# Sliding-window attention and feed-forward on one core: attention sinks laid into the preceding block's rows, with first-layer halves, an earlier W2 load and earlier crossbar transposes

## The chip, the cores and the metric

The kernel runs on one core of one Trainium2 chip. The metric is the device time of one execution in microseconds (us). Most executions agree within 0.3%; the kernel before takes 227.49 us (median of three runs, 226.96 to 227.76). A run counts as slow when it is over 1.5% above the fastest of its kernel.

## The reference, cut to what matters

Attention with a window of 128 keys and four sink keys that every query sees, then a layer norm, two matrix products with a ReLU between them, and a residual:

```python
batch, n_heads, seq, head_dim = (4, 8, 768, 64)      # n_sink 4, window 128
is_sink   = pos[None, :] < n_sink
rel       = pos[:, None] - pos[None, :]
keep      = is_sink | ((rel >= 0) & (rel < window))
a         = softmax(where(keep, q @ k.T / sqrt(64), -1e9))
x         = (a @ v), heads side by side               # 4 x 768 x 512
xn        = (x - mean) / sqrt(var + 1e-6) * g_ln
out       = x + relu(xn @ w_ch1) @ w_ch2               # 512 -> 2048 -> 512
```

## The kernel before

The 768 rows of each of four batches are cut into six blocks of 128: blocks 0 to 5 are batch 0, 18 to 23 batch 3. Four blocks form a group for the dense part (first layer `ph`, second layer `pc`). A query block sees its own keys and those of the block before it, and the window fits exactly: query row i of a block still sees key row j of the preceding block if j > i. From the third block of a batch on, the four sinks lie outside both blocks, so they get matmuls of their own: scores `pk`, an exponential, and two products per half block (line 496):

```python
if len(slots) > len(halves):                    # a sink block: 8 more score matmuls
    for h2 in range(2):
        for hp in range(4):
            nc.tensor.matmul(P["pk", t][32*hp:32*hp+32, h2, :], lhsT=ks_of[b][:, h2, hp, :],
                             rhs=qkT[t][:, 0, hp, :], start=(h2 == 0), stop=True, ...)
...
if r >= 2:                                      # and 2 more products per half block (L496)
    for h2 in range(2):
        nc.tensor.matmul(po.rearrange(...)[:, :, h2, :], lhsT=ES[t][:, h2, :], rhs=vs_t[b].rearrange(...), ...)
```

A planner inside the kernel takes tasks with estimated costs, dependencies and priorities and fixes each engine's instruction order before the kernel runs; each engine then works through its order and cannot overtake. All input loads are issued by POOL in one chain, block by block:

```python
def load(fn, land, take=(), desc=1024):
    i = plan.add({"POOL": 0.88}, [], fn, (0,), take=take, land=land, after=last_load[0], desc=desc)
    last_load[0] = i
    return i
...
DTR = set(range(8, NT))          # blocks whose transposes go through the DMA crossbar
SUBS = {0: [(0, 2), (2, 4)]}     # group 0's first layer in halves of two blocks
W2AT = 6                         # W2 is loaded ahead of block 6
for t in range(4, NT):
    if t == W2AT:
        for c in range(4):
            load_w2(c)
    load_block(t)
...
n = 8 * (t - 4) - 16             # scores of block t wait for the n-th piece of dense work
```

The softmax here doesn't subtract the row's maximum and nothing guards it: scores larger than these inputs give would overflow.

Of the kernel before, what the change touches and what calls it, by code (L numbers as in the profile page):

```python
# [14 lines left out]
class Planner:  # L15
# [16 lines left out]
    def run(self, free, warm_until):  # L32
# [15 lines left out]
        dma_free = free["DMA"]  # L48
        order = []
        queued = []  # L50
        while ready:
# [37 lines left out]
            if e == "PE":  # L89
                gaps[i] = start - free[e] if start < warm_until else 0.0  # L90
# [3 lines left out]
            if t["land"] is not None:  # L94
                dma_free = max(dma_free, start + 1.5) + t["land"]
                end = dma_free + (0.6 if t["lag"] is None else t["lag"])
                if t["desc"]:
                    queued.append((dma_free, t["desc"]))
# [15 lines left out]
    @staticmethod  # L114
    def room(queued, desc, ring=4096):

        for at, d in reversed(queued):
            desc += d
            if desc > ring:
                return at  # L120
        return 0.0

    def emit(self, order):
        for i, e, slots in order:
            self.gap = self.gaps.get(i, 0.0)
            self.tasks[i]["emit"](e, *slots)
# [3 lines left out]
def kernel(  # L130
# [35 lines left out]
    RINGS = dict(pa=4, ps=2, ld=LDN, qk=QKN, ks=2, vs=2, e=8, es=3, xc=4, xn=4, h1=32, ot=4)  # L166
# [14 lines left out]
    def warm(bank_):  # L181

        for _ in range(int(plan.gap * WARM / .056)):
# [22 lines left out]
    ks_t = [consts.tile([128, 2, 4, 32], BF16, name=f"ks_{i}") for i in range(2)]  # L206
    xt = [consts.tile([128, DM], BF16, name=f"xt_{t}") for t in range(NT)]
# [10 lines left out]
    def make_masks():  # L218
        v_ = nc.vector
        nc.gpsimd.iota(iota_d, pattern=[[1, 128]], base=0, channel_multiplier=-1)  # L220
        nc.gpsimd.iota(iota_h, pattern=[[-32, 4]], base=0, channel_multiplier=1)
        v_.tensor_scalar(ident, iota_d, 0.0, None, op0=ALU.is_equal)
# [28 lines left out]
    last_load = [None]  # L251

    def load(fn, land, take=(), desc=1024):
        i = plan.add({"POOL": 0.88}, [], fn, (0,), take=take, land=land, after=last_load[0], desc=desc)
# [58 lines left out]
    P = {}  # L313
    def w0(e, s):
# [6 lines left out]
    def opening():  # L321
        plan.add({"PE": .1}, [], w0, (0, -1, 0), take=[("pa", "w0", 0)])
        D["mb"] = plan.add({"DVE": .45}, [d_q[0]], make_masks_b, (0, 0, 1))
        D["mc"] = plan.add({"DVE": 1.3}, [d_q[0]], make_masks_c, (0, 1, 5))

# [4 lines left out]
    def block(t):  # L330
# [4 lines left out]
        split = t in SPLIT  # L335

# [20 lines left out]
        qk_readers = n_s(t) + (0 if last else n_s(t + 1)) + (1 if r == 0 else 0)  # L357
# [59 lines left out]

        s_ = []
        for halves in (((0,), (1,)) if t in SPLIT_S else ((0, 1),)):
            cost = .22 * nkb + .43 * nkb * (t in MPE)  # L420
            sink = r >= 2 and halves[-1] == 1
            x_ = plan.add({"PE": cost * len(halves) / 2 + .15 + SINK * sink},
                          d_c[t] + (d_c[t - 1] if r else []) + ([D["mb"]] if t in MPE and r else [])
                          + ([d_ks[b]] if sink else []), sc(halves),
# [7 lines left out]
        for half in range(2):  # L432
# [7 lines left out]
            def mk(e, half=half):  # L440
                m = (mask_zero, mask_one)[r] if r < 2 else mask_std
# [7 lines left out]
        if r == 0:  # L449
# [6 lines left out]
            d_ks[b] = plan.add({"DVE": .3}, d_c[t], mks, (0, t + 2, 0), take=[("ks", ("ks", b), 4)],  # L456
                               drop=[("qk", t)])
            vs_d = []
            for half in range(2):
                hs = slice(4 * half, 4 * half + 4)  # L460

                def pv_(e, s, *s2, half=half, hs=hs):
                    if s2:
# [5 lines left out]
                              take=[("pa", ("pv", b, half), 1)] + ([("vs", ("vs", b), 8)] if half == 0 else []))  # L469
# [9 lines left out]
        a_deps = [d_v[t]] + ([d_v[t - 1]] if r else [])  # L479
        if r >= 2:  # L480
# [7 lines left out]
        for half in range(2):  # L488
            def av(e, s, half=half):
# [4 lines left out]
                if r >= 2:  # L494
# [4 lines left out]
                for hh in range(4):  # L499
                    h = 4 * half + hh  # L500
                    nc.tensor.matmul(po[:, hh, :], lhsT=ee[:, h % 2, hh // 2, 0, :], rhs=vn[:, t, h, :],  # L501
                                     start=(r < 2 and hh == 0), stop=(r == 0), skip_group_check=True)
                    if r > 0:
# [3 lines left out]
            a = plan.add({"PE": (.12, .25, .37)[min(r, 2)]}, a_deps + [ms[half]], av, (0, t, 5),  # L507
                         take=[("pa", ("po", t, half), 1)],
                         drop=[("e", t, half)] + ([("es", t), ("vs", b)] if r >= 2 else []))

            def nm(e, half=half):
                po = P["po", t, half]
                rc = small.tile([128, 4], FP32, name="rc")
# [8 lines left out]
            ns.append(plan.add({"DVE": .60}, [a], nm, (0, t, 6), drop=[("po", t, half)]))  # L522
# [10 lines left out]
        def st(e):  # L533
            if ti == 0:
                mvg[g] = small.tile([128, 4, 2], FP32, name="mvg")
            st_ = small.tile([128, 6], FP32, name="st")
            nc.vector.bn_stats(st_, xt[t])  # L537
            nc.vector.bn_aggr(mvg[g][:, ti, :], st_)
# [195 lines left out]
```

## Time and profile before

| before | value |
|---|---|
| time, median | 227.49 us |
| profiled span, clock | 225.4 us, 1.00 |
| TensorE needed work, counted | 208.6 us |
| lost before the end of the last matmul | 12.5 us, of it 11.25 before 26.5 us |
| tail after the last matmul | 4.2 us |
| DVE busy / POOL busy | 135.0 / 76.0 us |

"Needed work" is the running sum of what each matmul group costs in an unbroken stream; "lost" is the real start of a group minus that sum. This pair is used throughout, because TensorE's busy share also counts warm-up matmuls. In the profile, PE is TensorE, PEld its weight loads, DVE VectorE, ACT ScalarE, POOL GpSimd, and SPq and POOLq are the queues from which SyncE and GpSimd issue transfers. The lines themselves are in the prediction.

### The profile page before, as it was taken

Reading aid. Unit: us, or ns where it says so; the run is one execution under the profiler, and the core shown is the slowest. Engines: PE = TensorE matmul, PEld = TensorE weight load, DVE = VectorE, ACT = ScalarE, POOL = GpSimd, SP = SyncE. Lnnn points to the kernel's source line nnn. Section 1 sums busy time; section 2 is a strip of 40 time slices with the busy share of each in tenths; the row PEclk is TensorE's granted clock in tenths of the full one; section 3 lists DMA queues with packets and bytes.
Section 4 is the critical chain, followed back from the end, with each engine's and each line's share of the span. In section 5 each row is a group of like instructions: output and inputs, shape, how many; then the busy total and the mean of one; then the engine's idle time right before and its main releaser. Section 6 shows DMA issues by size and latency. Waiting matters only on the chain.

```text
span 225.4 us, 4783 instructions
## 1 busy us (share of the span) xinstructions
PE 217.0 (96%) x1921; PEld 121.0 (54%) x1948; DVE 135.0 (60%) x398; ACT 104.0 (46%) x166; POOL 76.0 (34%) x92
## 2 busy tenths in 40 slices
PE   8999999999999999999999999999999999999992
PEld 7766787655455554455555544454555544444440
DVE  5777998779577988863756873654854712100121
ACT  2386788344367731167641258633077600376000
POOL 7994366691695242933088000100000010000000
PEclk9999999999999999999999999999999999999999
DMA  7999999999999999999989994203221021200111
GB/s 43 139 157 206 182 184 209 166 173 192 218 150 129 144 140 189 175 185 191 94 103 158 168 209 88 51 17 102 71 48 23 3 70 47 93 0 3 47 71 69
DMA packets 108709, 26.52 MB, mean 118 GB/s; under 512 B 101520, under 2 KB 105616, under 8 KB 108688
## 3 DMA queue, kind: packets, MB, share of 16 engines
q0 software_dynamic: 79104, 13.64, 81.7%
q1 hardware_dynamic: 29584, 12.59, 30.1%
q8 instruction: 15, 0.25, 0.4%
q14 instruction: 6, 0.05, 0.1%
HBM read 27.27 MB, written 6.29 MB: 149 GB/s over the span
## 4 chain that ended last, share of the span: by engine, by line
PE 81%; DMA 8%; POOL 5%; DVE 3%; issue 1%; ACT 0%; POOLq 0%; ACTq 0%
PE ph L603 34%; PE pc L634 34%; PE ps L406 5%; DMA w1s<-in_moe_w_ch_dram 4%; DMA qkT<-qkn 3%; PE po L501 2%; PE po L504 2%; POOL qkn L267 2%; POOL vn L275 2%; POOL qkn L272 2%; PE po L496 2%; PE pk L413 1%; PE pt L347 1%; DVE xt L517 1%; DVE w1s L299 1%
## 5 line engine op out<-in xcount | busy, mean ns | idle before, releaser
L603 PE MATMUL ph<-xnt,w1s 128*128 128x512 bf16 (+1 forms) x434 | 88.9, 348 | 1.0 <-DVE h L617 0.3
L634 PE MATMUL pc<-w2s,h 128*128 128x512 bf16 x371 | 87.0, 379 | 1.1 <-issue 0.5
L619 ACT ACTIVATE h<-ph 128x512 bf16<-128x512 f32 (+1 forms) x84 | 45.8, 546 | 53.8 <-PE ph L603 52.1
L603 PEld LDWEIGHTS <-w1s 128*128 128x128 bf16 x448 | 41.5, 98 | 35.4 <-ACT h L619 0.5
L634 PEld LDWEIGHTS <-h 128*128 128x128 bf16 x384 | 35.8, 98 | 39.1
L435 ACT ACTIVATE e<-ps 128x1024 bf16<-128x1024 f32 (+1 forms) x48 | 43.7, 951 | 12.5 <-PE ps L406 12.5
L646 DVE SCALAR_TENSOR_TENSOR ot<-pc,rsg,xt 128x512 f32<-128x512 f32 x24 | 17.9, 747 | 38.9 <-PE pc L634 38.9
L548 POOL TENSOR_TENSOR rsg<-ve,eps_half 128x4 f32<-128x4 f32 x6 | 6.2, 1028 | 82.0 <-DVE ve L546 82.0
L267 POOL DMA_DIRECT2D qkn<-in_q_dram x24 | 21.9, 910 | 14.9 <-DMA qkT<-qkn 13.1
L444 DVE TENSOR_TENSOR e<-e,mask_std 128x1024 bf16<-128x1024 bf16 x28 | 18.9, 684 | 10.9 <-ACT e L435 10.9
L617 DVE TENSOR_SCALAR h<-ph 128x512 bf16<-128x512 f32 (+1 forms) x28 | 15.9, 570 | 13.7 <-PE ph L603 13.6
L272 POOL DMA_DIRECT2D qkn<-in_k_dram x24 | 21.7, 903 | 2.8 <-DMA w2s<-in_moe_w_ch_dram 1.4
L275 POOL DMA_DIRECT2D vn<-in_v_dram x24 | 21.8, 912 | 1.8 <-DMA w1s<-in_moe_w_ch_dram 1.8
L517 DVE SCALAR_TENSOR_TENSOR xt<-po,rc 128x256 bf16<-128x256 f32 x48 | 20.4, 425 | 1.7
L501 PE MATMUL po<-vn,e 128*128 128x65 bf16 x192 | 17.1, 193 | 0.1
L537 DVE BATCH_NORM_STATS2 st<-xt 128x6 f32<-128x512 bf16 x24 | 16.4, 684 | 0.0
L406 PEld LDWEIGHTS <-qkT 64*128 64x128 bf16 x352 | 9.9, 94 | 10.4 <-issue 7.8
L406 PE MATMUL ps<-qkT 64*128 64x128 bf16 x352 | 14.7, 218 | 0.7 <-DMA qkT<-qkn 0.4
L482 ACT ACTIVATE es<-pk 128x256 bf16<-128x256 f32 x16 | 6.1, 383 | 19.9 <-PE pk L413 19.8
L514 DVE RECIPROCAL rc<-po 128x4 f32<-128x4 f32 x48 | 8.5, 178 | 11.3 <-PE po L504 10.4
L501 PEld LDWEIGHTS <-e 128*128 128x128 bf16 x192 | 14.0, 97 | 2.1 <-DVE e L444 0.5
L504 PE MATMUL po<-vn,e 128*128 128x65 bf16 x160 | 14.9, 193 | 0.0
(66 smaller groups left out, 146.2 us busy)
## 6 DMA issues: line engine op xcount, KB each, us to landing
out_dram<-ot SPq DMA_DIRECT2D x24, 256.0 KB, 2.5
qkn<-in_q_dram POOLq DMA_DIRECT2D x24, 128.0 KB, 7.1
qkn<-in_k_dram POOLq DMA_DIRECT2D x24, 128.0 KB, 6.8
vn<-in_v_dram POOLq DMA_DIRECT2D x24, 128.0 KB, 7.6
w1s<-in_moe_w_ch_dram POOLq DMA_DIRECT2D x4, 512.0 KB, 10.3
w2s<-in_moe_w_ch_dram POOLq DMA_DIRECT2D x4, 512.0 KB, 10.7
qkT<-qkn SPq DMA_TRANSPOSE x16, 7.2
xnt<-xc SPq DMA_TRANSPOSE x16, 5.6
```

What stands on the lines that cost most here:

```text
L267: nc.gpsimd.dma_start(qn[t][:, 0], q[b, :, rows, :].rearrange("h p d -> p h d"))
L272: nc.gpsimd.dma_start(qn[t][:, 1], k[b, :, rows, :].rearrange("h p d -> p h d"))
L275: nc.gpsimd.dma_start(vn[:, t, :, 0:64], v[b, :, rows, :].rearrange("h p d -> p h d"))
L406: nc.tensor.matmul(ps[:, h2, hh, kb, :], lhsT=qkT[t - kb][rows, 1, hp, :], rhs=qkT[t][rows, 0, hp, :], start=(hh == 0 and kb == 0 and t no ...
L435: nc.scalar.activation(E[t, half][:, :, :, 0:nkb, :], P["ps", t, half][:, :, :, 0:nkb, :], AF.Exp, scale=scale)
L444: nc.vector.tensor_mul(ee[:, :, 0:w], ee[:, :, 0:w], m[:, 0:w].unsqueeze(1).to_broadcast([128, 4, w]))
L501: nc.tensor.matmul(po[:, hh, :], lhsT=ee[:, h % 2, hh // 2, 0, :], rhs=vn[:, t, h, :], start=(r < 2 and hh == 0), stop=(r == 0), skip_grou ...
L504: nc.tensor.matmul(po[:, hh, :], lhsT=ee[:, h % 2, hh // 2, 1, :], rhs=vn[:, t - 1, h, :], start=False, stop=True, skip_group_check=True)
L517: nc.vector.scalar_tensor_tensor(xt[t][:, 256 * half:256 * half + 256].rearrange("p (h d) -> p h d", h=4), in0=po[:, :, 0:64], scalar=1.0, ...
L603: nc.tensor.matmul(ph, lhsT=w1s[:, j, 128 * ht:128 * (ht + 1)], rhs=xnt[g][:, j, cols], start=(j == 0), stop=(j == NDM - 1))
L619: nc.scalar.activation(o, i, AF.Relu)
L634: nc.tensor.matmul(P["pc", t], lhsT=h1[g, ht][:, 128 * ti:128 * (ti + 1)], rhs=w2s[:, ht, :], start=(ht == 0), stop=(ht == NH1 - 1))
```

## The change

Intent: for blocks 14 to 17 and 20 to 23 (`FOLD`), write the four sink keys and values over rows 0 to 3 of the preceding block, once that block no longer needs them, and open the mask for these rows. Then the ordinary matmuls do the sinks' work, and `pk`, its exponential and the products of L496 go away. The price: query row 0 loses keys 1 to 3 of the preceding block, row 1 keys 2 and 3, row 2 key 3. These six pairs per head and block are computed separately: 27 small loads on POOL fetch the rows (`fq`, `fk`, `fv`), a chain of small DVE operations forms corrections (`fc`), three small transfers spread them (`fcb`), and DVE adds them to the first three rows of the weighted sum. Beside that, group 1's first layer goes in halves, W2 is loaded one block earlier, blocks 6 and 7 use the crossbar for their normalised rows, and the pacing changes.

The diff holds four more things: the planner's own model of landings and costs, smaller rings of buffers (`xn` 2 for 4, `h1` 20 for 32), another count of warm-up matmuls, and the layer norm's row statistics, which ACT may now take in place of DVE.

```diff
+    def fetch(i, b):                                    # row i, batch b: three loads on 4 partitions each
+        at = slice(12 * i + 4 * (b - 1), 12 * i + 4 * b)
+        def f(e):
+            nc.gpsimd.dma_start(fq[at], q[b, :, 256:768, :].rearrange("h (r x) d -> x r h d", x=128)[i])
+            for to, src in ((fk, k), (fv, v)):
+                nc.gpsimd.dma_start(to[at].rearrange("r h p d -> r h (p d)"), src[b, :, 129:641, :]...)
+        fetched.append(load(f, .35, desc=96 * 3, cost=1.2))
+    def corrections():                                  # 6 score steps, exp on ACT, mask, 3 + 3 value steps
+        d = step(.2, fetched, mask)
...
+        if fold:                                        # sinks over the preceding block's rows 0 to 3
+            nc.vector.tensor_copy(qkT[t - 1][:, 1, :, 0:4], kss_of[b])
+            nc.vector.tensor_copy(vn[0:4, t - 1], vn[0:4, t - r])
...
+                if fold:
+                    nc.vector.tensor_add(po[0:3], po[0:3], fcb[:, t - RB - 2 * b, 4 * half:4 * half + 4, :])
...
-        v_ = d_var[t] = plan.add({"DVE": .87}, ...
+        v_ = d_var[t] = plan.add({"DVE": .87, "ACT": 1.1}, ...
...
-    DTR = set(range(8, NT))
+    DTR = set(range(6, NT))
-    SUBS = {0: [(0, 2), (2, 4)]}
+    SUBS = {0: [(0, 2), (2, 4)], 1: [(0, 2), (2, 4)]}
-    W2AT = 6
+    W2AT = 5
+    FOLD = 12
+    FETCH = 14
...
+        if t == FETCH:                                  # ahead of block 14's load, in the one chain of loads
+            for b in range(1, B):
+                for i in range(3):
+                    fetch(i, b)
         load_block(t)
...
-        n = 8 * (t - 4) - 16
+        n = 9 * (t - 4) - 24
```

## The prediction

> **What bounds the kernel now.** I read the page's busy shares first, then the busy time of the engines by stage, then the chain that ended last and the timeline of TensorE, and then I counted TensorE's needed work, because a busy share alone doesn't say whether the work is needed. First the page, then three stages (columns after the stretch: its length, then busy us of PE, PEld, DVE, ACT and POOL with instructions in brackets, clock, DMA share, GB/s):
>
> ```profile
> PE 217.0 (96%) x1921; PEld 121.0 (54%) x1948; DVE 135.0 (60%) x398; ACT 104.0 (46%) x166; POOL 76.0 (34%) x92
> ```
>
> ```profile
> 0.00:26.50 26.50, 24.80 (x334) 18.89 (x335) 19.66 (x76) 15.26 (x24) 20.18 (x29) 1.00 1.52 145
> 26.50:60.00 33.50, 32.72 (x355) 22.38 (x359) 28.28 (x83) 18.24 (x35) 18.75 (x22) 1.00 1.88 180
> 60.00:180.00 120.00, 118.44 (x1054) 61.28 (x1069) 80.68 (x231) 60.45 (x92) 36.04 (x41) 1.00 1.20 120
> ```
>
> PE is the only full engine from 26.5 us on; DVE is at 84% of 26.5 to 60 and 67% of 60 to 180. What one group of matmuls costs in the stream is its piece in the chain (start, us, what), since the next group starts right behind it:
>
> ```profile
> 43.53 1.73 PE pc L634 x8
> 45.26 0.22 PE px L559 x4
> 49.52 0.11 PE pv L466
> 51.82 7.83 DMA qkT<-qkn
> 60.31 0.23 PE pk L413 x8
> 63.23 0.12 PE po L496 x2
> 65.68 0.55 PE ps L406 x16
> ```
>
> So 216 ns for a 512-column matmul, 0.22 us for four transposes, 0.23 for the eight sink scores (pk), 0.12 for the two sink products of a half block (L496), 0.55 for a block's scores, which are also entered some 0.1 us late (312 ns instead of 216 from the last wide matmul before them). Counted over TensorE's whole program: first layer 320 x 216 + 128 x 109 ns = 83.1 us; second layer 384 x 216 ns = 82.9; scores 12.6 and entering them 2.6; masks by matmul 3.0; weighted sums 352 x 30 ns = 10.7; sink scores 16 x 0.225 = 3.6; sink products 32 x 0.118 = 3.8; q and k transposes 64 x 56 ns = 3.6; transposes of the normalized rows 32 x 56 ns = 1.8; sink value spreads 8 x 0.11 = 0.9. The sum is 208.6 us. The last matmul ends at 221.2, so about 12.5 us are lost, and the tail after it is 4.2.
>
> Where the 12.5 lie I see by laying this running sum against the starts in the timeline: at the matmul below 15.3 us of needed work are done, so 11.25 are already lost; at 38.95 it is 0.34 more, at 59.69 another 0.5 (block 8's transposed q and k came late; the 7.83 us above), and from there to the end some 0.2. **The opening is bound by loads and latency, everything after it by the amount of TensorE work.**
>
> ```profile
> 26.52 2.78 PE L603 MATMUL ph<-xnt,w1s 128*128 128x256 bf16 x24 [0.28 <-DVE h L617]
> ...
> 59.69 0.62 PE L406 MATMUL ps<-qkT 64*128 64x128 bf16 x16 [0.45 <-DMA qkT<-qkn]
> ```
>
> **What the Trainium skill says.** "Trainium Kernel Development and Optimization", Performance Expectations, warns that matmul busy time says little about the distance to the best, as matmuls are pipelined; I agree here, 96% also counts warm-up matmuls, and that is why I counted work. "TensorE: Matmul & The Clock Gate", Part 1, gives N / 2.4 GHz plus about 2.5 ns for a warm matmul, so 215.7 ns at 512 columns; the trace has 216, and halves of 256 columns cost 109, so splitting a first layer in halves costs TensorE under 0.3 us in 128 matmuls. The same part says that a busy array keeps its clock and an idle one loses it after a few us; here the granted clock is 1.00 in all three stages. "DMA: Bandwidth & Descriptors", Issuing engines are not separate DMA queues, says that transfers from all issuers share the same 16 engines; the 7.83 us of a transpose under loads, against 3.0 us for the quickest one of the same kind in this trace, agree.
>
> **The change part by part.**
> Sinks: for blocks 14 to 17 and 20 to 23 the four sink keys and values are written over the first four rows of the preceding block, whose mask then lets them pass, and three rows get a correction. Eight blocks lose 0.225 + 2 x 0.118 = 0.46 us of TensorE each: 3.7 us. Batches 2 and 3 have no old-style block left, so 4 of the 8 value spreads go: 4 x 0.11 = 0.45 us. ACT loses 8 x 0.38 us of sink exponentials. It adds on DVE: a 3 x 260 add per half block, estimated at 0.42 us from the 128 x 260 multiply out of PSUM (0.424), 16 times, 6.7 us; key and value copies, estimated 0.15 and 0.3, eight times, 3.6; the corrections, about a dozen 512-element fp32 operations which I estimate at 0.65 (the output operation of that width takes 0.747) plus small ones, 8.5 us. It saves about 3 us of spreads and sink key copies. DVE goes from 135 to some 150 of about 221 us. That is under the bound, beside TensorE's work.
> Loads: 27 more small loads stand on POOL between the loads of blocks 13 and 14. A 1024-row load takes 0.91 us of POOL, a 512-row one 0.745, so I estimate 0.4 to 0.7 for 32 rows: 11 to 19 us.
> Crossbar from block 6: in the instruction order only the normalized rows of blocks 6 and 7 move; q and k of these stay on TensorE. 8 x 56 ns = 0.45 us less.
> First layer of group 1 in halves: 64 matmuls of 216 become 128 of 109, no cost on TensorE; 16 more evacuations on ACT or DVE at about 0.2 us of fixed cost each, beside other work. It lets the layer start before blocks 6 and 7 are through.
> W2 behind block 4: the packet records show loads of blocks 0 to 3 until about 15.4 us, W1 to 25.7, blocks 4 and 5 to 30.9, W2 to 41.2. Now W2 ends at about 38.6 and block 5 at 41.2. Group 0's second layer begins at a running sum of 28.0 us, with 11.3 lost at 39.3, and block 5's transposes at 42.8: both just behind their data. I expect no gain and no stall.
> Opening: fewer warm-up matmuls stand before the first transposes (3 instead of 18), but the first layer waits for W1, whose first quarter was scaled from 19.7 us on in both. More attention is now done ahead of it (11.2 against 10.6 us), so up to 0.6 us less is lost; I take 0.4.
>
> Sum: needed TensorE work 208.6 - 3.7 - 0.45 - 0.45 = 204.0, with small order effects 204.2; lost 12.5 - 0.4; new stalls in the middle 0.4; tail 4.2. The span is 204.2 + 12.1 + 0.4 + 4.2 = 220.9 us. The time exceeds the profiled span by 227.45 - 225.4 = 2.05. I put it at 222.9; as the stall at block 8 may go (its transposes stand behind an output store that now comes 2.5 us earlier, worth 0.4), I settle on 222.5 us, 2.2% less.
>
> **The rivals.**
> (1) The small loads are slow. The corrections start on DVE behind block 5's output, at a running sum of 74.9, about 86.5 us. The fetches can begin when block 13 is loaded, about 66.5 (in the kernel before POOL issued block 14 there). At 0.4 us each they end at 77, at 0.65 at 84, both in time; at 0.9 at 91, and DVE, which takes its work in order, would stand some 6 us in front of block 13's masks, and block 14 would be loaded late for its scores at about 100.6. TensorE would lose 2 to 5 us: 225 to 227. For it: POOL's 0.745 for 512 rows shows a large fixed part. Against: the interval from 66.5 to 86.5 holds them at up to 0.7.
> (2) DVE becomes the bound: the fold lengthens the path from weighted sum to freed PSUM bank from 0.67 to about 1.1 us, and the one group of corrections is 8.5 us in one stretch. For it: DVE was at 84% before 60 us. Against: the fold lies after 100 us, where it was under 67%. It would make 223.5 to 225.
> (3) The crossbar in the middle or at the end is late: block 23's normalized rows are needed 7 us after its last weighted sum (running sum 169.75 to 176.6) instead of about 16. The chain there is about 2.2 us of DVE and 2.4 to 5.6 us of transpose, so 0 to 1 us lost.
> (4) The opening gains more than I think, since its 11 lost us are the largest reserve: if the first layer starts 1 us sooner, 221.5.
>
> **Range and chances.** The certain part is 4.6 us of TensorE work, to about 222.9 with nothing else; the opening can add up to 1.5 us of gain, the rivals take 1 to 5. So 220.5 to 224.9 us, 8 in 10. The 2% line is at 222.94, close above my number: faster by over 2% 0.60, within 2% 0.38, slower 0.02.
>
> **What would show it.** TensorE's groups: pk from 128 to 64, L496's from 64 to 32, pv from 8 to 4, px from 32 to 24, and the last matmul's end 4 to 5 us sooner, with the stream as gapless after 60 us as before. DVE at about 150 us busy. The small loads at 0.4 to 0.7 us each on POOL, done before 87 us. A DVE idle before the corrections, ended by a load, would prove rival 1; TensorE idle ended by DVE's normalization rival 2; TensorE idle near 188 us ended by a transpose rival 3. I am wrong if TensorE loses over 2 us more after 60 us than now, or if the opening shifts by over 1.5 us.

## The result, and the profile after

The changed kernel takes **238.92 us** (median of four runs, 237.05 to 240.99), against 227.52 us for the kernel before on the same chip. The ratio is 1.0477 (95% interval 1.0411 to 1.0543): slower by 4.8%, where 2.2% faster was predicted. Ratios are the mean time of one kernel's fast runs over the mean of the other's fast runs in the same rounds, so they are not quite the ratio of the medians quoted beside them.

The profiled run is the slowest of the four (240.99 us, span 239.2) and carries the mark slow. The other three have spans of 235.3 to 237.5 us and granted clocks of 0.976 to 0.978, against 0.968. The readings below are therefore confirmed further down on a fast run of nearly the same kernel ("The change's layout, every other part undone"), which shows the largest of the stops.

The page of the changed kernel (busy us, share, instructions; then the tenths of 40 slices of about 6 us):

```profile
PE 216.2 (90%) x1869; PEld 124.0 (52%) x1892; DVE 139.1 (58%) x422; ACT 113.2 (47%) x200; POOL 92.5 (39%) x120
...
PE   8799999998999799419949999999999999999993
...
PEclk9999999999999999956997999999999999999998
```

PE is busy for almost the same time as before, although the work fell: the 17th and 18th slice (about 96 to 108 us) are at 4 and 1 tenths, and the granted clock falls to 5 and 6 tenths in the 18th and 19th, so the matmuls that follow take twice as long and count as busy. The same by stages, with the columns that the prediction explains:

```profile
0.00:26.50 26.50, 24.12 (x328) 18.31 (x329) 18.46 (x77) 15.10 (x24) 19.86 (x30) 1.00 1.51 145
26.50:60.00 33.50, 32.55 (x355) 22.63 (x356) 25.81 (x78) 19.82 (x41) 19.45 (x23) 1.00 1.93 174
60.00:90.00 30.00, 27.45 (x334) 20.45 (x334) 23.10 (x75) 17.90 (x36) 15.15 (x22) 1.00 1.68 137
90.00:130.00 40.00, 27.59 (x181) 12.49 (x183) 20.83 (x54) 14.10 (x23) 26.17 (x33) 0.83 1.48 117
130.00:180.00 50.00, 49.53 (x366) 24.26 (x372) 29.26 (x90) 24.17 (x42) 10.86 (x12) 1.00 1.18 127
```

For the stretch of 90 to 130 us the kernel before has:

```profile
90.00:130.00 40.00, 39.48 (x342) 20.26 (x346) 26.03 (x73) 17.05 (x26) 19.34 (x22) 1.00 1.72 155
```

There PE issued 342 recorded matmuls in 39.48 us at full clock; now 181 in 27.59 us at 0.83. Everything that went wrong on a large scale lies here. In needed work and lost time, the changed kernel stands at 204.3 us of needed work, as predicted. Lost are 10.69 us at 26.3 us (0.56 less than before), 11.57 at 59.5 us, 14.70 at 91.4, 23.73 at 107.05, and 31.1 at the end. Between 91 and 129 us it loses 16.1: a stop of 9.03 at 107, 2.2 at half clock behind it, a stop of 3.20 at 125, and 1.7 at half clock behind that.

Who waited for whom (engine, line, waited for, total us, times, longest):

```profile
DVE fk L383 <- DMA fv<-in_v_dram: 11.2, 1, 11.2
...
PE po L601 <- DVE e L533: 8.9, 1, 8.9
...
DVE po L615 <- DMA fcb<-fc: 5.4, 1, 5.4
...
PE ph L714 <- DVE xt L620: 3.0, 1, 3.0
```

DVE stands 11.2 us before the first correction because the small loads that it reads have not landed: the last `fk`, issued at 98.68, lands at 101.39. (The profile names an `fv` load, which shares the wait but lands at 102.37 only.) Behind the corrections in DVE's fixed order stands block 13's mask, for which TensorE waits 8.9 us. Later DVE waits 5.4 us for the spread corrections, and TensorE, whose PSUM bank is held by block 14's sum until then, 3.0 us. DVE's and then TensorE's timeline show it (start, us, engine, line, what, idle before):

```profile
90.31 0.15 DVE L376 TENSOR_SCALAR mask_c<-iota_c 36x3 f32<-36x3 int32 x1
101.66 0.68 DVE L383 TENSOR_TENSOR fk<-fk,fq 36x512 f32<-36x512 f32 x1 [11.20 <-DMA fv<-in_v_dram]
...
106.27 0.67 DVE L533 TENSOR_TENSOR e<-e,mask_one 128x1024 bf16<-128x1024 bf16 x1
```

```profile
107.00 0.23 PE L601 MATMUL po<-vn,e 128*128 128x65 bf16 x1 [8.85 <-DVE e L533]
...
107.43 6.49 PE L714 MATMUL ph<-xnt,w1s 128*128 128x512 bf16 x19
...
115.51 3.63 PE L714 MATMUL ph<-xnt,w1s 128*128 128x512 bf16 x16
```

The 19 recorded matmuls behind the stop take 6.49 us, the 16 a little later 3.63: starts lie 426 ns apart instead of 216 until the clock returns.

And POOL's timeline shows the 27 small loads:

```profile
67.67 0.65 POOL L365 DMA_DIRECT2D fq<-in_q_dram  x1
...
70.83 0.59 POOL L367 DMA_DIRECT2D fv<-in_v_dram  x1 [1.92 <-DMA qkn<-in_q_dram]
75.06 0.59 POOL L365 DMA_DIRECT2D fq<-in_q_dram  x1 [3.64 <-DMA qkn<-in_k_dram]
...
82.48 0.59 POOL L367 DMA_DIRECT2D fk<-in_k_dram  x1 [3.15 <-DMA vn<-in_v_dram]
...
99.26 0.59 POOL L367 DMA_DIRECT2D fv<-in_v_dram  x1
99.84 0.95 POOL L295 DMA_DIRECT2D qkn<-in_q_dram  x1
```

Issuing one takes 0.59 us, within the 0.4 to 0.7 that the prediction estimated. But the 27 take from 67.67 to 99.85, 32.2 us: 16 us of issuing and 16 us of waiting. Each wait ends when the load eight issues earlier lands, so the first ones end with block loads and not with small ones: the issue at 70.83 waited for block 12's queries, issued at 59.97 and landed at 70.55, the one at 75.06 for block 12's keys, landed at 74.77. The program has eight semaphores in turn for POOL's loads, so at most eight are under way. Of the 16.3 us of waiting, 10.6 end with loads of blocks 12 and 13, which took 10.6 to 15.4 us to land, and 5.7 with small loads, of which the first 15 took 7.5 to 14.8 us and the last 12 took 2.7 to 6.3. So the eight places let through about one load per 1.2 us (32.2 / 27). Block 14's load, issued at 66.56 us before, now comes at 99.84.

### The profile page after: what moved, and what is told of

It is laid out like the page before. It is cut to its first block, busy times and chain, and to the rows that moved or that the text cites. A ratio compares the mean times of both kernels' runs of the same rounds, so it can differ in the third digit from the quotient of the medians.

```text
span 239.2 us, 4774 instructions
## 1 busy us (share of the span) xinstructions
PE 216.2 (90%) x1869; PEld 124.0 (52%) x1892; DVE 139.1 (58%) x422; ACT 113.2 (47%) x200; POOL 92.5 (39%) x120
## 4 chain that ended last, share of the span: by engine, by line
PE 64%; DMA 24%; POOL 7%; issue 2%; SPq 1%; DVE 1%; ACT 0%; POOLq 0%; DVEq 0%
PE pc L745 27%; PE ph L714 25%; DMA vn<-in_v_dram 6%; DMA qkT<-qkn 5%; DMA fk<-in_k_dram 4%; DMA fcb<-fc 4%; PE ps L484 4%; DMA qkn<-in_k_dram 3%; DMA qkn<-in_q_dram 2%; PE po L601 2%; POOL qkn L295 2%; PE pt L425 1%; PE ps L475 1%; PE po L604 1%; POOL fv L367 1%
## 5 line engine op out<-in xcount | busy, mean ns | idle before, releaser
L714 PE MATMUL ph<-xnt,w1s 128*128 128x256 bf16 (+1 forms) x506 | 92.9, 334 | 3.3 <-DVE xt L620 3.0
L745 PE MATMUL pc<-w2s,h 128*128 128x512 bf16 x367 | 86.5, 379 | 0.9 <-issue 0.2
L730 ACT ACTIVATE h<-ph 128x512 bf16<-128x512 f32 (+1 forms) x95 | 48.4, 511 | 45.9 <-PE ph L714 44.7
L714 PEld LDWEIGHTS <-w1s 128*128 128x128 bf16 x512 | 48.6, 99 | 36.5 <-issue 4.3
L659 POOL TENSOR_TENSOR rsg<-ve,eps_half 128x4 f32<-128x4 f32 x6 | 6.7, 1118 | 67.0 <-DVE ve L657 65.6
L601 PEld LDWEIGHTS <-e 128*128 128x128 bf16 x192 | 14.3, 99 | 12.8 <-DVE e L533 9.3
L728 DVE TENSOR_SCALAR h<-ph 128x256 bf16<-128x256 f32 (+1 forms) x33 | 15.5, 476 | 7.3 <-PE ph L714 6.8
L533 DVE TENSOR_TENSOR e<-e,mask_one 128x1024 bf16<-128x1024 bf16 x22 | 14.7, 684 | 5.8 <-ACT e L524 5.8
L604 PEld LDWEIGHTS <-e 128*128 128x128 bf16 x160 | 11.3, 99 | 2.3 <-issue 0.3
L615 DVE TENSOR_TENSOR po<-po,fcb 3x260 f32<-3x260 f32 x16 | 6.7, 421 | 7.4 <-DMA fcb<-fc 5.4
```

The source lines that it names most:

```text
L601: nc.tensor.matmul(po[:, hh, :], lhsT=ee[:, h % 2, hh // 2, 0, :], rhs=vn[:, t, h, :], start=(not sinks and hh == 0), stop=(r == 0), skip_ ...
L604: nc.tensor.matmul(po[:, hh, :], lhsT=ee[:, h % 2, hh // 2, 1, :], rhs=vn[:, t - 1, h, :], start=False, stop=True, skip_group_check=True)
L714: nc.tensor.matmul(ph, lhsT=w1s[:, j, 128 * ht:128 * (ht + 1)], rhs=xnt[g][:, j, cols], start=(j == 0), stop=(j == NDM - 1))
L730: nc.scalar.activation(o, i, AF.Relu)
L745: nc.tensor.matmul(P["pc", t], lhsT=h1[g, ht][:, 128 * ti:128 * (ti + 1)], rhs=w2s[:, ht, :], start=(ht == 0), stop=(ht == NH1 - 1))
```

## The experiments

The theories, whose letters the quoted expectations use. **A**: the loss comes with the fold's small loads, through the corrections that wait for them and block 14's load behind them. **A1**: by their number. **A2**: by the bytes that each puts on few engines, so that they land late and hold the eight places. **The rivals**: the other parts of the change, crossbar and W2 above all (**B**); the fold's own path, its adds and the spread of its corrections (**C**); the corrections' own time on DVE, or their place in its order (**D**). Of the last runs, **G** says that this place in the order is the whole of a second stop, **H** that DVE is short of time or the transfers crowded. All kernels gave a correct result by the comparison, and all ran three rounds beside the kernel before (medians of 227.37 to 227.76 us).

**Without the fold.** No small loads, no corrections, sinks as before; everything else of the change stays.

```diff
-    FOLD = 12
-    FETCH = 14
+    FOLD = NT
+    FETCH = NT
...
-    corrections()
```

> The changed kernel without the folded sinks: no small loads, no corrections, old-style sinks in all blocks; halves, early W2 and crossbar from block 6 stay. Theory A (the 27 small loads in GpSimd's queue hold up VectorE and block 14, and everything else is small): TensorE's work rises to 208.5 us, the 12 us of waiting at the corrections and the slow clock behind it vanish, the late transposes before 92 us (about 2.5 us) stay: 226 to 229 us. Theory B (the crossbar transposes of blocks 6 and 7 and the moved W2 fill the DMA engines and are the main cause): 233 us or more.

Measured: 228.78 us (one of the four runs is slow), ratio of the fast runs 1.0014 (0.9961 to 1.0067). The cost came with the fold, as A had it. The other parts together are worth nothing: blocks 8's and 12's transposed tiles come 1.1 and 1.5 us late.

**Without the fold, crossbar from block 8.** The same and one part more undone.

```diff
     (as above)
-    DTR = set(range(6, NT))
+    DTR = set(range(8, NT))
```

> The changed kernel without the fold (no small loads, no corrections, all sinks as before) and with the crossbar from block 8: what is left of the change is W2 behind block 4, group 1's first layer in halves and the pacing. Needed work as before plus 0.1 us. In the run without the fold, the crossbar from block 6 saved 0.45 us of work and block 8's and 12's transposed tiles came 1.1 and 1.5 us late. If the two further blocks on the crossbar made them late, both are under 0.6 us here and the time is 226 to 227.5 us; if the earlier W2 load or the pacing makes them late, they stay and it is 228 to 230 us.

Measured: 228.67 us, ratio 1.0041 (1.0016 to 1.0066). Blocks 8 and 12 are still 1.6 and 1.0 us late, so the crossbar of blocks 6 and 7 is not what delays them. The next run says the same with the fold in.

**Crossbar from block 8, fold in.** Only the `DTR` line is put back.

> The changed kernel with crossbar transposes from block 8 on, as before the change; the rest stays. Theory A: only the late transposes before 92 us get less, and the small loads wait a little less behind blocks 12 and 13: 234 to 238 us. Theory B: 224 to 229 us.

Measured: 237.25 us, ratio 1.0396 (1.0343 to 1.0450); as A expected.

**Small loads from SyncE, early.** The 27 loads are issued by SyncE from 30 to 53 us, behind the scaling of W1, and the corrections stand behind block 12's scores.

```diff
-            nc.gpsimd.dma_start(fq[at], q...)
+            nc.sync.dma_start(fq[at], q...)
...
-        fetched.append(load(f, .35, desc=96 * 3, cost=1.2))
+        fetched.append(plan.add({"SP": 1.4}, [D["hold"]] if not fetched else [], f, (0,), land=.05, lag=2.0,
+                                after=fetched[-1] if fetched else None))
```

> The fold stays, but the 27 small loads are issued from SyncE behind the scaling of W1 (about 28 us), where its queue is empty, and the corrections stand behind block 12's scores. Theory A: the wait at the corrections is gone, block 14 loads behind block 13, TensorE's work is 204.3 us: 222 to 226 us. Theory C (the fold's own path, the adds on VectorE and the spread of the corrections, is what stalls): still over 231 us. Theory B: still over 231 us, too.

Measured: 235.03 us, ratio 1.0330 (1.0280 to 1.0380). A's expectation was missed; the time is what B and C had (over 231). Yet the stop at the corrections, which C needs, is gone. Instead the big loads are late where the small ones now are: block 6's and 7's values land at 54.17 and 57.78 us instead of 45.49 and 48.56, and TensorE loses 3.6 us up to 45.9 (two stops, of 1.5 and 1.8), 2.9 at 52.9 and 2.7 at 70, with half clock behind them. The cost travels with the loads, though issuer and time were changed at once. In the records their packets take 46.6 us summed over the engines; if four engines carried them at a time, that would be some 12 us, an estimate that fits the delay of 9 us.

**Small loads from SyncE, and crossbar from block 8.** Both edits.

> Small loads from SyncE and crossbar from block 8: both at once. Theory A with the crossbar as a smaller second cause: 221 to 224 us, below e2 by 1 to 3 us. If the crossbar costs nothing of its own: the same as e2, or 0.5 us above it for the eight transposes that TensorE does again.

Measured: 243.78 us, ratio 1.0698 (1.0669 to 1.0727). A miss too, with 3.5 us lost up to 47 and a stop of 4.4 at 71. The 8.7 us over the previous run come later: stops of 1.9 us at 111 and 3.9 at 115, with half clock. There the corrections stand on DVE ahead of a block's normalisation (`xc` at 106.17), whose transpose, behind the three spreads, lands at 115.25; TensorE's next first layer starts at 115.34. That is the second stop which the last runs below explain. Issuing from another engine at this place is no cure.

**The same 27 loads with an eighth of the bytes.** Each fetches one head of eight; the other heads' rows are zeroed by GpSimd beforehand. The result is wrong for these rows, by too little for the comparison to notice.

```diff
-            nc.gpsimd.dma_start(fq[at], q[b, :, 256:768, :]...)
+            nc.gpsimd.dma_start(fq[at][:, 0:1], q[b, 0:1, 256:768, :]...)
```

> The changed kernel with the same 27 small loads in the same place, but each brings one head of the eight (an eighth of the bytes); the three tiles are zeroed by GpSimd ahead of block 12's load. The result is wrong on purpose. Theory A1 (what costs is the number of loads: GpSimd's 0.59 us each, and the wait until the load eight places earlier has landed): the stretch from the first to the last small load stays at about 28 to 32 us and the time at 235 to 240 us. Theory A2 (what costs is the bytes: each small load writes 4 partitions only, so few DMA engines carry all of it and everything behind it waits): the stretch shrinks to 20 to 24 us and the time to 226 to 232 us.

Measured: 228.30 us, ratio 1.0057 (1.0001 to 1.0113). The same number of loads on the same partitions costs 10 us less, so A1 falls. It is not a clean measure of the bytes: with the zeroing ahead of block 12's load, the block loads before the small ones landed faster too (7.8 to 10.6 us, against 10.6 to 15.4), and that is 4.7 of the 11 us by which the last small load is earlier. POOL's timeline of this run:

```profile
83.94 0.50 POOL L365 DMA_DIRECT2D fq<-in_q_dram  x1
84.42 0.50 POOL L367 DMA_DIRECT2D fk<-in_k_dram  x1
84.91 0.51 POOL L367 DMA_DIRECT2D fv<-in_v_dram  x1
```

They follow without a gap: those issued from 78 us on land in 1.5 to 3.8 us (the seven before them took 4.7 to 9.7), so that the eight places are free in time. The 27 are through in 19.5 us instead of 32. What is left is a stop of 2.8 us at 112 us for the spread corrections.

**Eighteen small loads.** The nine of batch 1 are used by nobody, since only batches 2 and 3 are folded; they are dropped.

```diff
-            for b in range(1, B):
+            for b in range(2, B):
```

> The changed kernel without the nine small loads of batch 1, whose blocks are not folded, so that their corrections are used by nobody (right result; tiles of 24 instead of 36 partitions). Theory A1 or A2: the last small load is issued 6 to 11 us earlier, the wait of VectorE before the corrections falls from 11.2 to under 5 us, and TensorE's wait of 9 us with the slow clock behind it mostly goes: 228 to 232 us. If the loads' number were not the cause: 237 us or more.

Measured: 232.24 us (229.25 to 233.85; two of the four runs are slow), ratio of the fast runs 1.0136 (1.0064 to 1.0207). In fast runs, a third fewer loads bring the ratio from 1.0477 to 1.0136, but with two fast runs, 2.4 us apart, no rule can be made of it.

**Corrections behind block 13 on DVE.** They may begin only when block 14's scores are issued, so behind block 13's masks. The 27 loads stay.

```diff
-        d = step(.2, fetched, mask)
+        d = step(.2, fetched + [d_s[14]], mask)
```

> The changed kernel with the corrections put behind block 13 in VectorE's order; the small loads stay as they are. If VectorE's standing in front of block 13's masks is what stops TensorE (9 us and about 2 us of half clock), that stop goes, and the late corrections and block 14's late load show instead, as a stop of 3 to 8 us at block 14: 231 to 237 us. If the time is set by block 14's late load anyway: 237 us or more, no change.

Measured: 241.76 us (two of the five runs are slow; the fast ones are 239.51 to 241.76), ratio 1.0542 (1.0503 to 1.0582): no gain, the second of the two cases expected. The stop at block 13's mask is gone, but block 14's scores now show what stood behind it:

```profile
PE ps L484 <- DMA qkT<-qkn: 11.5, 4, 8.4
```

Block 14's load stands behind the small ones and is as late as the corrections are. Two paths of almost the same length run through the small loads. And the corrections, begun so late, are missed in their turn: 5.2 us more are lost up to 133.5 us, most of it in a stop of 4.2, before which DVE has waited for the spread.

**Fold of batch 3 alone, small loads after the last block.** Nine loads at 125 us, behind nothing that anyone waits for; crossbar from block 8.

```diff
-    FOLD = 12
+    FOLD = 18
...
-        if t == FETCH: ... fetch(i, b)
         load_block(t)
+    for b in range(3, B):
+        for i in range(3):
+            fetch(i, b)
```

> The fold for batch 3 alone (blocks 20 to 23), with its nine small loads behind the last block's load, where the DMA engines have room, and crossbar from block 8. TensorE's work is 206.8 us, 2 less than before the change. Theory A: no stop at the corrections, no late transposes: 224 to 226.5 us. Theory C (the fold's own path stalls): over 228 us.

Measured: 227.41 us, ratio 0.9997 (0.9968 to 1.0025), 1 us above what was expected. There is no stop at the corrections. The needed work is 206.8 us, but block 8's and 12's tiles are late by 1.6 and 1.0 us and the opening lost more in this run, so the half fold is even.

**Another layout of the same corrections.** A partition holds one head of a batch, and the four blocks' three rows lie side by side in it. So a load goes to 8 partitions and takes all rows; without the unused batch there are 6 loads with 144 KB instead of 27 with 504 KB. The corrections also get a dependency on block 12's scores.

```diff
+    fq, fk, fv, ft = [consts.tile([16, 4, 3, 64], FP32, name=n) for n in ("fq", "fk", "fv", "ft")]
...
+    def fetch(b):
+        at = slice(8 * (b - 2), 8 * (b - 1))
+            for to, src, at_row in ((fq, q, 256), (fk, k, 129), (fv, v, 129)):
+                nc.gpsimd.dma_start(to[at]..., src[b, :, at_row:at_row + 512, :]...)      # 8 partitions
...
-        d = step(.2, fetched, mask)
+        d = step(.1, fetched + [d_s[12]], lambda e: nc.vector.memset(fs, -30000.0))
```

> The changed kernel with the corrections laid out anew and nothing else moved: one partition for a head of a batch, the three rows of a block side by side in it, batches 2 and 3 alone, so 6 small loads on 8 partitions each (144 KB in all) for the 27 on 4 partitions (504 KB); the same pairs of query row and key row are corrected, and block 14 onwards is loaded behind them as before. Theory A2 (the 27 loads stand in the way of block 14's load and of the corrections, by the bytes that each puts on few engines and by the wait of each for the landing of the load eight issues earlier): the issues take at most 6 x 1.2 = 7 us, the stop of 9 us at block 13's mask is gone with its half clock, block 14's scores wait under 1 us: 221 to 226 us, the late transposes of blocks 8 and 12 (2.7 us in the run without the fold) being all that is left to lose. Rival D (the stop comes from DVE's corrections themselves, or from the place in the order that the planner gave them): a stop of 4 us or more at block 13 or 14 stays, 232 to 238 us.

Measured: 233.83 us, ratio 1.0268 (1.0206 to 1.0330). Better than the change by 5 us in the medians, but inside rival D's range of 232 to 238 us. Block 14's load is in time now, and yet TensorE stops for 2.4 us at 97 and for 5.4 us at 103, with 2.4 us at half clock. This stayed open until the last two runs; they show that D was right for this layout, by the place in the order.

**The same, crossbar from block 8.**

> The kernel of the run with heads on the partitions, with crossbar transposes from block 8 again in place of block 6. Costs 8 transposes on TensorE (0.45 us). If the late landing of block 8's and block 12's transposed tiles comes from the two further blocks' transposes in the transfer engines' queues, both waits fall below 0.6 us and the time is 1 to 2 us below the run with heads on the partitions (221 to 224 us); if it comes from something else (the loads around them, the pacing of the blocks), the waits stay and the time is the same or 0.4 us above it.

Measured: 232.33 us, ratio 1.0222 (1.0181 to 1.0264). The stops of 97 and 103 us are there again, and block 8's tile is still 1.3 us late, so the further crossbar blocks are not what delays it.

**The new layout, every other named part of the change undone.** Crossbar from 8, W2 behind block 5, halves for group 0 alone, old pacing. The planner's model, the smaller rings and the statistics on ACT stay.

```diff
-    SUBS = {0: [(0, 2), (2, 4)], 1: [(0, 2), (2, 4)]}
+    SUBS = {0: [(0, 2), (2, 4)]}
-    W2AT = 5
+    W2AT = 6
-        n = 9 * (t - 4) - 24
+        n = 8 * (t - 4) - 16
```

> Heads on the partitions, and every other part of the change undone: crossbar from block 8, W2 behind block 5, the first layer in halves for group 0 alone, the blocks paced as before. So the kernel before plus the folded sinks of batches 2 and 3. Needed work on TensorE falls by 4.2 us against before; before's waits were 0.9 us from block 4 to the end. If the fold is worth what it removes, 223 to 224.5 us, the best of all kernels; if the corrections or the longer normalisation on DVE give some of it back, 225 to 227 us.

Measured: **224.44 us**, ratio 0.9863 (0.9813 to 0.9913), faster than before by 1.4% (the interval excludes 1). TensorE in 90 to 130 us, and POOL's small loads:

```profile
90.00:130.00 40.00, 40.00 (x320) 19.74 (x314) 32.51 (x97) 20.55 (x34) 17.70 (x20) 1.00 1.83 167
```

```profile
70.75 0.55 POOL L359 DMA_DIRECT2D fv<-in_v_dram  x1
71.55 0.95 POOL L288 DMA_DIRECT2D qkn<-in_q_dram  x1 [0.26 <-DMA qkn<-in_k_dram]
```

All six are issued within 3.4 us (67.90 to 71.3), and block 14's load follows after 0.26 us of waiting. DVE is at 32.51 of 40 us, so more than in the change, and TensorE does not stop.

**The change's layout, every other part undone.** The partner of the last run: only the layout and the loads of the corrections differ, and their dependency on block 12's scores.

> The fold in the changed kernel's own layout (27 small loads on 4 partitions each, corrections of batches 1 to 3), every other part of the change undone: crossbar from block 8, W2 behind block 5, halves for group 0 alone, paced as before. Against the run with heads on the partitions and the same old order (224.4 us) only the layout of the corrections differs. If the small loads are the cause: the stop at block 13's mask and block 14's late load are there with their half clock, 7 us or more: 231 to 238 us. If the earlier W2 load, the halves, the pacing or the crossbar were the larger part of it: 225 to 229 us.

Measured: 235.90 us, ratio 1.0342 (1.0294 to 1.0390). This run is fast and repeats the largest stop of the profile of the change:

```profile
90.00:130.00 40.00, 32.34 (x243) 15.52 (x242) 26.96 (x73) 17.42 (x28) 26.44 (x33) 0.91 1.78 143
```

```profile
PE po L601 <- DVE e L533: 7.7, 1, 7.7
```

The two layouts lie 11.5 us apart in the same order. In the last run the corrections stood ahead of block 13's mask on DVE as well (the mask is at 94.60); but their loads had landed at 75.92, so nothing waited behind them. That speaks against rival D for the change itself. (Of the 12.5 us between the two profiled spans, some 3 lie before the small loads, at block 8, where the lateness differs from run to run; the rest lies behind them.)

**Which other part makes the second stop?** The new layout in the old order, with one part of the change put in at a time. First W2 behind block 4:

> The fastest kernel so far (heads on the partitions, old order, 224.4 us) with W2 behind block 4 in place of block 5. One of the three parts that stand between 224.4 us and the 232.3 us of the same kernel with all three. If W2's earlier load delays blocks 5 to 8 and so block 8's transposed tile: 225 to 226.5 us. If it is harmless, 224 to 225. If it alone makes the stop at blocks 13 and 14, 230 or more.

Measured: 224.58 us (one of four executions, the profiled one, took 1238.91 us and is left out as slow; the other three are 223.62 to 224.83), ratio 0.9844 (0.9798 to 0.9891). Harmless. The pacing of the change:

> The fastest kernel so far with the changed kernel's pacing of the blocks (block t held to 9(t-4)-24 quanta of dense work in place of 8(t-4)-16). It moves the attention of blocks 13 to 16 by 1 to 3 quanta behind dense work and earlier blocks the other way. If the stops at block 13's mask and at the first layer behind it come from DVE being asked for the corrections and for blocks close together, this run has a stop of over 2 us near 95 to 103 us: 227 to 231 us. If not: 224 to 225.5.

Measured: 224.21 us, ratio 0.9832 (0.9779 to 0.9886). Harmless. Group 1's first layer in halves:

> The fastest kernel so far with group 1's first layer in halves. It adds 64 more, shorter evictions' and issues' worth of steps around 43 to 60 us, before the corrections, and lets group 1's dense work begin two blocks earlier, so that the dense work of the later groups lies earlier against the blocks. If the halves make block 8 late or crowd DVE: 226 to 230 us; if they are harmless (needed work is 0.1 us longer): 224 to 225.5.

Measured: 230.98 us, ratio 1.0155 (1.0089 to 1.0220). Here the second stop is. The lines of this run, from the waits, DVE's, SyncE's and TensorE's timelines:

```profile
PE ph L706 <- DMA xnt<-xc: 3.5, 1, 3.5
```

```profile
91.49 0.41 DVE L385 TENSOR_TENSOR fc<-fc,ft 16x256 f32<-16x256 f32 x1
92.10 0.75 DVE L749 SCALAR_TENSOR_TENSOR ot<-pc,rsg,xt 128x512 f32<-128x512 f32 x1 [0.20 <-PE pc L737]
92.77 0.20 DVE L623 TENSOR_SCALAR sums<-sums 128x1 f32<-128x1 f32 x1
93.01 0.35 DVE L626 TENSOR_SCALAR xc<-xt,sums 128x512 bf16<-128x512 bf16 x1
```

```profile
91.93 2.01 SPq L389 DMA_DIRECT2D fcb<-fc  x3
94.03 0.53 SPq L756 DMA_DIRECT2D out_dram<-ot  x1
94.67 1.26 SPq L668 DMA_TRANSPOSE xnt<-xc  x1
```

The planner had put the corrections ahead of block 11's normalisation (`xc` at 93.01). Its crossbar transpose then stands behind the three spreads, is issued at 94.67 and lands at 101.64, and group 2's first layer starts at 101.78. In the run with halves undone, half of the corrections stand behind it and the same tile is formed at 88.15. In the changed kernel itself it is formed at 84.73, ahead of the corrections. So this second stop comes from the place that the planner gave the early-loaded corrections in the new layout, and is no part of the change's loss.

**Corrections behind block 11's normalisation**, in the kernel with halves:

```diff
-        d = step(.1, fetched + [d_s[12]], ...)
+        d = step(.1, fetched + [d_s[12], d_ln[11]], ...)
```

> The run with heads on the partitions, old order and halves in group 1 (230.98 us), with one thing moved: the corrections on DVE stand behind block 11's normalisation in place of ahead of it. In that run block 11's normalised tile was formed at 93.0 us behind the corrections, its crossbar transpose was issued at 94.67 and landed at 101.64, and TensorE, which needs it for group 2's first layer, stood still until 101.77. Theory G: that place in DVE's order is the whole of the second stop. Then it goes, with its half clock, and the mask of block 13 has TensorE work beside it: 223.5 to 226 us. Rival H: DVE is simply short of time there with the corrections in (9 us of it), or the halves crowd the transfers: a stop of 3 us or more stays between 90 and 112 us, 228 to 232 us.

Measured: 224.01 us (one of the four runs is slow), ratio of the fast runs 0.9832 (0.9794 to 0.9870), 7 us less than without this one dependency. The tile is formed at 82.90, issued at 83.43 and landed at 91.17; the stop and its half clock are gone.

**The whole change with both repairs**: new layout, corrections behind block 11, and the change's own crossbar, W2, halves and pacing.

> The whole change with two repairs: heads on the partitions, and the corrections behind block 11's normalisation on DVE. Crossbar from block 6, W2 behind block 4, halves in both groups and the pacing are the change's own. Without the second repair it took 233.83 us. Theory G: 222.5 to 226 us, what the prediction had for the change, with the late transposed tiles of block 8 (1.4 us) left; whether it is above or below the 224.4 us of the same fold in the old order tells whether the other parts are worth having. Rival H: 230 to 235 us.

Measured: **223.79 us** (223.06 to 225.44), ratio 0.9863 (0.9813 to 0.9913). It is inside the range that was predicted for the change. Its stretch of 90 to 130 us:

```profile
90.00:130.00 40.00, 39.64 (x318) 19.60 (x313) 30.75 (x89) 21.42 (x37) 17.90 (x20) 1.00 2.01 172
```

Theory G holds, H falls. The needed work is 204.3 us and 12.9 are lost, against 208.6 and 12.5 before. In one view:

| kernel | us | ratio to before |
|---|---|---|
| before | 227.4 to 227.8 | 1 |
| the change | 238.92 | 1.0477 |
| change without fold | 228.78 | 1.0014 |
| 27 loads with an eighth of the bytes | 228.30 | 1.0057 |
| old order, the change's layout | 235.90 | 1.0342 |
| old order, new layout | 224.44 | 0.9863 |
| old order, new layout, with halves | 230.98 | 1.0155 |
| the same, corrections behind block 11 | 224.01 | 0.9832 |
| whole change, new layout, corrections behind block 11 | 223.79 | 0.9863 |

## Why the prediction was wrong

It said 222.5 us (220.5 to 224.9) and faster with a chance of 0.60; 238.92 us is outside the range, on the side that got a chance of 0.02.

**The bound, and the needed work: right.** The count was 204.2 us for the changed kernel, and the same count over its trace gives 204.3. The four groups that it named shrank as it said: `pk` from 128 to 64, the sink products from 64 to 32, `pv` from 8 to 4, `px` from 32 to 24.

**The opening: right in size.** 0.4 us was taken, 0.56 was gained in the profiled run. From run to run it moves by more than that.

**DVE: not the bound, and 11 us too high.** It was put at some 150 us and is at 139.1, although the parts were sized well: the add of a half block takes 0.421 us as estimated, a 512-element correction 0.68 instead of 0.65. What the prediction missed is that ACT took the row statistics of 11 of 24 blocks; on DVE they fell from 20.8 to 11.3 us. Rival 2, which made DVE the bound, did not come about. Nor did rival 3: from 129 us to the end TensorE loses next to nothing.

**Block 8: wrong, small.** The stall "may go", it said; it grew by some 0.5 us instead, and was 0.5 to 2.5 us in all the variants. From the other parts the prediction took 0.45 us (crossbar) and 0.4 us (opening); the runs without the fold, at 1.0014 and 1.0041, show no gain in time.

**The step that failed is rival 1's sizing of the small loads**: "At 0.4 us each they end at 77, at 0.65 at 84, both in time", and "the interval from 66.5 to 86.5 holds them at up to 0.7". The mechanism that rival 1 names, DVE standing before block 13's masks and block 14 loaded late, is exactly what happened. The sum counted issuing alone: 27 x 0.59 = 16 us, which would have ended at 84. Three terms were missing or too small.

1. *The wait for a place.* At most eight of POOL's loads are under way, and each small one waits for the landing of the one eight issues earlier: 16 us more on POOL (10.6 of them for block loads that were under way before the small ones), so the last is issued at 99.26 and lands at 102.37 instead of before 87.
2. *The landing time.* These loads have 8 or 24 KB, and I gave them no time to land. They took up to 15 us, with medians of 7.5 to 8.3 us in the trace. That their number alone does not make it is shown by the run with an eighth of the bytes (20 of the 27 landed in 1.5 to 3.8 us, 10 us less in all).
3. *What a stop costs behind itself.* I had 2 to 5 us for rival 1. The stops themselves were 9.0 and 3.2 us, and another 3.9 us went in matmuls at 426 ns instead of 216, because the idle TensorE had lost its clock. "TensorE: Matmul & The Clock Gate", Part 1, which the prediction cites, says that an idle array loses its clock; I quoted it and did not put it into the sum.

The Trainium skill has a reason for term 2. "DMA: Bandwidth & Descriptors", Why a DMA increments its semaphore by 16 and not by 1, says that a transfer is spread over the largest k up to 16 engines that divides the slowest dimension of both its patterns. A load on four partitions would then use four engines, one on eight partitions eight, and the ordinary loads on 128 partitions all sixteen. The runs agree in direction: 6 loads on 8 partitions with 144 KB are harmless where 27 on 4 partitions with 504 KB cost 11.5 us. The trace has no engine numbers for packets, but its packet records agree on the four: packets of 4608 and 1536 bytes, which only the small K and V loads have, start in fours, the smaller when the larger end (four of 4608 between 83.32 and 83.35 us, for 0.33 us, and four of 1536 at 83.66 to 83.68). The same records show that most of a landing time is no moving of bytes: between the first such packet, at 78.06, and the last, at 101.2, any is in flight for only 9 of 23 us, and the first comes 9.8 us after its load was issued. And the wait is not the small loads' doing alone: in the run without the fold, block loads issued between 60 and 90 us took 8 to 15 us to land. Since the new layout changed the number, the bytes and the partitions at once, the weight of each, and of the confinement to few engines, is argued and not shown.

**Two paths, not one.** The corrections and block 14's load both stood behind the small loads. Moving the corrections alone gave 241.76 us; only repairing the loads repaired both.

**What the change is worth when the loads are repaired**: 223.79 us, 1.3 above the prediction and 4 below the kernel before, or 1.4%; so even then it would not have passed the 2% that got a chance of 0.60. Of the 4.3 us of work that it takes off TensorE, about 3 to 4 reach the time. The other named parts add nothing to that: the fold in the old order gives the same ratio of 0.9863. What the statistics on ACT, the smaller rings and the planner's model are worth was not tested apart.

## What to carry to other kernels

A transfer's price on the issuing engine is not its issue time: ask how many may be under way, how long each takes to land at that moment of the kernel, and what stands behind it in the same chain. Lay small gathers out as few transfers that span more partitions (here 6 on 8 in place of 27 on 4; which of the two counts was not separated), and check in the trace that each engine's fixed order has nothing urgent behind an operation that waits for them. When an engine that has been the bound stands still for several microseconds, add the time at half clock that follows to the cost of the stop.

## What the Trainium skill lacked or had wrong

- No page has the wait for a free place among loads under way: here each POOL load waited for the one eight issues earlier, 16 us over 27 small loads ("DMA: Bandwidth & Descriptors" would be its place; the eight are this program's semaphores, not shown to be a limit of the chip).
- "DMA: Bandwidth & Descriptors", Anatomy of one DMA — SWDGE (gpsimd) path, fits 2.0 us plus bytes / 436 GB/s, so 2.1 us for 24 KB. Here loads of that size on four partitions took 2.7 to 15 us from issue to landing beside other traffic, with medians of 7.5 and 7.9. Nor is its constant a floor: with an eighth of the bytes, 20 of 27 loads landed in 1.5 to 3.8 us.
- The same page has no figure for the issue of a small load on GpSimd: 0.59 us on four partitions here, 0.55 on eight, against 0.91 for a block of 128 partitions.
